# Attention scores in column tiles of 32 keys, with later queries only, in a recurrent-attention and MoE kernel

## The chip, the cores and the metric

One core of a Trainium2 chip runs the whole program. The metric is device time in microseconds (us) of that core; the kernel before took 594.9 us (median of 3 runs, 594.86 to 596.61). TensorE (PE in the profile) multiplies matrices into PSUM, VectorE (DVE), ScalarE (ACT) and GpSimd (POOL) work on tiles, and the sync engine (SP) issues the DMA transfers.

## The reference

Stage one is a linear recurrence with a complex decay, for 4 batches, 8 heads, 768 steps and 48 dimensions; stage two is a feed-forward layer over all 3072 tokens.

```
for t in range(S):
    new_re = ar * S_re - ai * S_im          # ar, ai: normalised decay of step t
    new_im = ar * S_im + ai * S_re
    S_re, S_im = new_re + outer(k[t], v[t]), new_im
    y[t] = q[t] @ S_re
x = y, heads side by side                   # [3072, 384]
h = x @ w_in                                # [3072, 2048]
g = maximum(h, 0) + log1p(exp(-abs(h)))
out = g @ w_out                             # [3072, 384]
```

The kernel computes stage one in 24 chunks of 128 steps (6 groups of steps times 4 batches). Within a chunk, query t sees key s only where s <= t, so the matrix of scores is triangular; what lies before the chunk comes in through a state.

## The kernel before

**Per chunk and in order.** `pre` turns the decays into logarithms and angles (ACT and DVE), sums them along the steps (matmuls L508 for the first group, scans L491 later), and multiplies q and k with the resulting powers; DMAs L603 and L607 copy q and k into the tile qk, with the 96 real and imaginary parts of a head on the partitions. `chunk` then does, for each of the 24 chunks:

- transposes of k (PE L622), evacuated by ACT (L629, L631);
- scores (PE L647): for each of 8 heads one f32 matmul of 128 keys by 128 queries, four heads into one PSUM bank, so two halves of four matmuls;
- the mask (DVE L650): each half times a 128x128 triangle of ones, into the tile a;
- the output y (PE L678 from the state, L681 from a and v): 16 matmuls each, of 32 columns of weights, four of them side by side in the array's four column tiles;
- the new state (PE L703, in three column tiles, and DVE L712).

**The feed-forward layer.** `moe` runs per group of 512 tokens: for each of 16 slices f of d_ff, nine matmuls of 512 columns into h (L738), then Abs, Exp, Ln on ACT (L743 to L745), three DVE operations (L746, L748, L750; the second also on ACT, L749), and nine matmuls into three accumulators o (L762). A tile is split into a rounded part and a rest (gh and gl, xh and xl), hence nine instead of three. There are 96 groups of nine of each kind. From here on a group means nine such matmuls.

**A check.** `inspect` loads both weights once more in 32 pieces (seen), takes their absolute value (ACT L393) and sums up a bound (ACT L394); `judge` then weighs all the bounds (DVE L863 to L867), adds them up with a 1x1 matmul pn (PE L871) and so decides whether a slower general path is needed. It isn't here.

**What sets the order.** Nothing is ordered by the program text: every operation is a task with a cost, dependencies and a key from the table `K`, and `Planner.order` plays the engines through and writes out one order per engine, which the engines follow strictly. Where PE has nothing ready before the first group of L762, the planner writes a filler, a matmul of the identity (L798), so that PE's clock stays up. The number of fillers is thus fixed when the program is built.

Of the kernel before, what the change touches and what calls it, by code (L numbers as in the profile page):

```python
# [11 lines left out]
F32 = mybir.dt.float32  # L12
# [4 lines left out]
ALU = mybir.AluOpType  # L17
# [4 lines left out]
P = 128  # L22
B, H, S, D = 4, 8, 768, 48
# [5 lines left out]
CH = 128  # L29
# [14 lines left out]
KVT = 32  # L44

# [18 lines left out]
class Buf:  # L64
    def __init__(self, pool, tag, shape, dtype, name, bufs=1):
# [5 lines left out]
    def __call__(self):  # L71
        if self.obj is None:
            self.obj = self.pool.tile(self.shape, self.dtype, tag=f"{self.tag}_{self.slot}", name=self.name, bufs=1)
        return self.obj


class Task:
    __slots__ = ("eng", "dur", "fn", "key", "idx", "deps", "outs", "bufs", "tab", "nbytes", "left", "ready", "end", "alt")

    def __init__(self, eng, dur, fn, key, idx, tab, nbytes):  # L80
        self.eng, self.dur, self.fn, self.key, self.idx, self.tab, self.nbytes = eng, dur, fn, key, idx, tab, nbytes
        self.deps, self.outs, self.bufs, self.end = set(), [], [], 0.0
        self.alt = {}


class Planner:
    WIN = 3.4133
    FREE = 0.2
    LAT = {"ACT": {"ACT": 0.14, "DVE": 0.14, "PE": 0.15, "POOL": 0.1, "SP": 0.1},
# [45 lines left out]
    def order(self, filler, until, gate):  # L135
# [36 lines left out]
        table = "log"  # L172
        out = []
# [3 lines left out]
        while done < n:  # L177
# [20 lines left out]
            for e in engines:  # L198
# [4 lines left out]
                for t in pend[e] + (alts[e] if e in alts else []):  # L203
                    if t.ready > now:
                        nxt = t.ready if nxt is None else min(nxt, t.ready)
                        continue
                    if not room(t):
                        continue
                    if e == "SP" and dma_free > now + K["backlog"]:
                        nxt = dma_free - K["backlog"] if nxt is None else min(nxt, dma_free - K["backlog"])  # L210
                        continue
                    if t.eng != e:
                        work = max(0.0, free[t.eng] - now) + sum(
                            u.dur for u in pend[t.eng] if u.ready <= now and (u.key, u.idx) < (t.key, t.idx))
                        if work + t.dur < t.alt[e][0] + K["altpen"]:
                            continue
                    k = t.key + (K["tpen"] if t.tab and t.tab != table else 0.0)
                    if best is None or (k, t.idx) < best[0]:
                        best = ((k, t.idx), t)
                if best is None and e == "PE" and ends and gate.end and not until.end:  # L220
                    t = Task("PE", 0.214, filler, 0, -1, None, 0)
                    free[e] = now + self.array(now, t.dur)
# [22 lines left out]
                if e == "PE":  # L245
                    dur = self.array(now, dur)
# [31 lines left out]
class Prog:  # L278
# [15 lines left out]
    def consts(self):  # L294
# [4 lines left out]
        self.mask = c.tile([P, P], F32, tag="mask", name="mask")  # L299
        nc.gpsimd.memset(self.mask, 1.0)  # L300
        nc.gpsimd.affine_select(
            out=self.mask, in_=self.mask, pattern=[[1, P]], base=0,
            channel_multiplier=-1, compare_op=ALU.is_ge, fill=0.0,
        )
# [93 lines left out]
    def pre(self, si):  # L398
# [176 lines left out]
    def chunk(self, si, c):  # L575
# [13 lines left out]
        vt = self.vt[gc]  # L589
# [47 lines left out]
        am = []  # L637
        for j in range(2):
# [29 lines left out]
        def ymm():  # L668
            yy, q, v = y(), qk(), vt()
# [14 lines left out]
        add("PE", 1.19 if first else 2.38, ymm, at(), r=[qk, vt] + am + ([] if first else [sp]), w=[y])  # L684
# [9 lines left out]
        if not last:  # L694
# [11 lines left out]
            add("PE", 0.95, kvmm, at("state"), r=[kt, vt], w=[kv])  # L706
# [93 lines left out]
    def fast(self):  # L800
        with ExitStack() as ctx:
# [3 lines left out]
            self.x, self.vt = {}, {}  # L805
# [151 lines left out]
    def tokens(self):  # L957
# [78 lines left out]
    "judge": 3656.994,  # L1036
    "head": [
        2361.764, 90.426, 186.918, 828.6, -1179.026, 1665.811, 853.645, 122.5, 210.292, 299.959,
        2514.528, 765.795, 773.157, 1145.396,
    ],  # L1040
    "turn": [
        -1513.703, 2539.75, 283.981, -99.814, 144.317, 2815.741, 2230.689, 133.705, 205.779, 204.008,
        499.374, 774.09, 741.541, 373.819,
    ],
    "tail": [
        -5848.997, 383.858, -1999.396, -642.154, -5.741, 2629.094, 285.386, 132.423, 999.968, 189.692,
        228.801, 4092.001, 4909.0, 4392.766,
    ],
    "chunk": [
        -918.284, -524.779, 2957.251, 1802.451, 205.193, 104.187, 2951.945, 1167.349, 960.729, 1177.829,  # L1050
        4197.869, 270.781, 852.91, 259.323, 2229.167, 587.025, 439.879, 286.542, 2159.076, 855.741,
        1181.943, 2905.977, 1810.108, 1955.233,
    ],
    "state": [
        -3231.394, -1499.995, -99.254, -124.602, 43.116, 43.124, 88.757, 55.237, 128.405, 128.491,
        135.783, 136.063, 199.792, 140.866, 242.533, 203.435, 281.062, 250.568, 287.24, 301.809,
        -219.968, 2830.189, 43.882, -576.403,
    ],
    "wgt": [
        -470.753, -1307.379, 346.43, -3791.449, -3420.177, -1988.745, 2456.441, 389.871, 1190.129,  # L1060
        117.907, 129.074, 312.459, 123.09, 417.712, 146.793, 741.91,
    ],
    "moe": [
        31.451, 83.853, 132.162, 198.126, 302.101, 1104.311, 4399.954,
    ],
    "step": [
        4.077, 3.163, 2.754, 6.265, 4.251, 185.005, 1662.331,
    ],
    "seen": 116.978,
    "seenstep": 583.073,  # L1070
    "rlead": 357.33,
    "xlead": -5880.358,
    "vlead": -78.682,
    "plead": -5.114,
    "backlog": 1.983,
    "altpen": -0.151,
    "tpen": 10.226,
# [19 lines left out]
def _layout(q, k, v, a_re, a_im, moe_w_in, moe_w_out):  # L1097
# [23 lines left out]
    vpad = np.ascontiguousarray(vp.reshape(B, NGRP, CH, VW).transpose(2, 1, 0, 3).reshape(CH, NCHUNK, VW))  # L1121
# [20 lines left out]
```

## Time and profile before

| | |
|---|---|
| median of 3 runs | 594.9 us |
| profiled execution | 595.1 us |
| its span | 593.3 us |
| PE busy | 573.6 us, 97% of the span |
| weight loads (PEld) busy | 477.9 us, 81% |
| DVE busy | 438.2 us, 74% |
| ACT busy | 439.4 us, 74% |
| HBM read, written | 50.33 MB, 5.51 MB |

The span runs from the first to the last instruction of the program; 1.8 us of the profiled execution's time lie around it. A matmul's busy time in the profile overlaps with the next one's, so what a matmul costs PE is read from start to start. An f32 matmul leaves two records in the trace, an fp32r one (L738, L762) one.

### The profile page before, as it was taken

The page shows a single profiled execution, that of the slowest core. Times are in us where ns is not written, and L with a number is a line of the kernel's source. Part 1 is how long each engine was busy: PE and PEld are TensorE (multiplying, and loading weights), DVE is VectorE, ACT ScalarE, POOL GpSimd, SP SyncE. Part 2 cuts the span into 40 slices and gives each one's busy share as a digit, 9 for nine tenths or more (in the row PEclk, how much of TensorE's full clock was granted, in tenths as well). Part 3 has the DMA queues.
Part 4 walks back from the last instruction along what each step waited for, and adds up shares of the span by engine and source line. Part 5 has one row for each costly group of instructions (what it writes and reads, how often), then busy time and mean ns, then how long its engine had stood idle before and what let it go on. Part 6 is the DMA issues. An engine that isn't in the chain of part 4 may idle for free.

```text
span 593.3 us, 12166 instructions
## 1 busy us (share of the span) xinstructions
PE 573.6 (97%) x4984; PEld 477.9 (81%) x4984; DVE 438.2 (74%) x676; ACT 439.4 (74%) x770; POOL 1.8 (0%) x16
## 2 busy tenths in 40 slices
PE   1999999999999999999999999999999999999995
PEld 1999988887887888788888888888888877788884
DVE  6998998978997999886967978877735335443432
ACT  7987688658989597858859668699549899365452
POOL 1000000000000000000000000000000000000000
PEclk9999999999999999999999999999999999999999
DMA  8899743424002527244431434510329973010001
GB/s 325 345 299 297 304 123 124 112 75 155 1 0 68 163 74 225 69 128 156 124 123 29 111 124 108 176 43 27 81 60 301 296 223 110 2 53 1 0 1 57
DMA packets 42237, 75.55 MB, mean 127 GB/s; under 512 B 3520, under 2 KB 26560, under 8 KB 42176
## 3 DMA queue, kind: packets, MB, share of 16 engines
q1 hardware_dynamic: 42176, 74.73, 40.7%
q8 instruction: 40, 0.66, 0.5%
q14 instruction: 21, 0.17, 0.1%
HBM read 50.33 MB, written 5.51 MB: 94 GB/s over the span
## 4 chain that ended last, share of the span: by engine, by line
PE 74%; DVE 11%; ACT 9%; DMA 3%; issue 1%; SPq 1%; DVEq 0%; ACTq 0%
PE h L738 27%; PE o L762 26%; PE o L798 6%; PE sc L647 5%; PE y L681 2%; PE kv L703 2%; PE y L678 2%; PE tr L622 2%; DVE lt L746 2%; PE sum L508 1%; DVE gl L750 1%; DMA seen<-w_out_dram 1%; DVE a L650 1%; DVE x L531 1%; ACT L850 1%
## 5 line engine op out<-in xcount | busy, mean ns | idle before, releaser
L738 PE MATMUL h<-xt,wi 128*128 128x512 f32 x864 | 218.8, 399 | 0.8 <-DVE lt L746 0.7
L762 PE MATMUL o<-gh,wo 128*128 128x512 f32 x576 | 198.0, 400 | 0.0
L738 PEld LDWEIGHTS h<-xt,wi 128*128 128x128 f32 x864 | 159.7, 188 | 38.1 <-DVE lt L746 1.9
L746 DVE SCALAR_TENSOR_TENSOR lt<-h,lt 128x512 f32<-128x512 f32 x96 | 66.1, 689 | 99.3 <-ACT lt L745 99.1
L762 PEld LDWEIGHTS o<-gh,wo 128*128 128x128 f32 x576 | 108.4, 188 | 25.7 <-issue 1.2
L743 ACT ACTIVATE lt<-h 128x512 f32<-128x512 f32 x96 | 56.7, 592 | 81.9 <-PE h L738 81.4
L762 PE MATMUL o<-gl,wo 128*128 128x512 f32 x288 | 113.8, 395 | 0.1
L745 ACT ACTIVATE lt<-lt,one 128x512 f32<-128x512 f32 x96 | 69.5, 724 | 2.2
L750 DVE TENSOR_TENSOR gl<-lt,gh 128x512 fp32r<-128x512 f32 x96 | 66.2, 689 | 2.2 <-ACT gh L749 0.6
L762 PEld LDWEIGHTS o<-gl,wo 128*128 128x128 f32 x288 | 54.3, 188 | 12.1 <-DVE gl L750 0.6
L744 ACT ACTIVATE lt<-lt 128x512 f32<-128x512 f32 x96 | 60.6, 631 | 2.0
L647 PE MATMUL sc<-qk 96*128 96x128 f32 x384 | 48.4, 278 | 0.3 <-DVE a L650 0.3
L647 PEld LDWEIGHTS sc<-qk 96*128 96x128 f32 x384 | 46.2, 191 | 3.0 <-DVE a L650 0.7
L798 PE MATMUL o<-ident 128*128 128x128 f32 x334 | 40.3, 278 | 0.0
L798 PEld LDWEIGHTS o<-ident 128*128 128x128 f32 x334 | 39.1, 194 | 0.2 <-issue 0.2
L650 DVE TENSOR_TENSOR a<-sc,mask 128x512 f32<-128x512 f32 x48 | 32.2, 684 | 9.4 <-PE sc L647 9.2
L491 DVE TENSOR_TENSOR_SCAN t<-hold,t 128x384 f32<-128x384 bf16 x40 | 36.1, 945 | 1.1 <-DMA out_dram<-o 0.4
L850 ACT ACT_TABLE_LOAD x28 | 35.9, 1283 | 0.4
L749 ACT ACTIVATE gh<-lt 128x512 fp32r<-128x512 f32 x40 | 25.2, 630 | 11.3 <-DVE lt L746 7.1
L748 DVE TENSOR_SCALAR gh<-lt 128x512 fp32r<-128x512 f32 x56 | 23.9, 426 | 3.9
L681 PE MATMUL y<-a,v 128*32 128x128 f32 x768 | 25.9, 273 | 0.0
L564 DVE TENSOR_TENSOR x<-x,t 128x768 f32<-128x768 f32 x24 | 22.3, 952 | 4.3 <-ACT t L538 4.2
(88 smaller groups left out, 607.4 us busy)
## 6 DMA issues: line engine op xcount, KB each, us to landing
x<-dense_dram SPq DMA_DIRECT2D x20, 768.0 KB, 5.8
qk<-x SPq DMA_DIRECT2D x48, 288.0 KB, 4.2
raw_wo<-w_out_dram SPq DMA_DIRECT2D x8, 768.0 KB, 10.0
raw_wi<-w_in_dram SPq DMA_DIRECT2D x8, 768.0 KB, 7.8
seen<-w_in_dram SPq DMA_DIRECT2D x16, 384.0 KB, 4.3
seen<-w_out_dram SPq DMA_DIRECT2D x16, 384.0 KB, 3.8
v<-vpad_dram SPq DMA_DIRECT2D x24, 224.0 KB, 2.6
qk<-x SPq DMA_DIRECT2D x48, 96.0 KB, 3.9
```

Source lines behind the costliest of these rows:

```text
L647: PE.matmul(psc()[:, hh * P : (hh + 1) * P], q[:, h, CH:], q[:, h, :CH], start=True, stop=True)
L650: V.tensor_tensor(a(), psc().rearrange("p (h t) -> p h t", h=4), self.mask[:, None, :].to_broadcast([P, 4, P]), ALU.mult)
L681: PE.matmul(o(G), v[:, w : w + 32], am[h // 4]()[:, h % 4, :], start=first and prim and G < 4, stop=not prim)
L738: PE.matmul(h()[:, :n], w()[:, q, i, fs], x()[:, i, :n], start=k == 0, stop=k == 3 * NI - 1)
L743: add("ACT", a1(n) - 0.04, lambda: A.activation(tv(), h(), AF.Abs), k, r=[h], w=[t])
L744: add("ACT", a1(n), lambda: A.activation(tv(), tv(), AF.Exp, scale=-1.0), k, w=[t], tab="log")
L745: add("ACT", a1(n, 1), lambda: A.activation(tv(), tv(), AF.Ln, bias=self.one), k, w=[t], tab="log")
L746: add("DVE", d1(n), lambda: V.scalar_tensor_tensor(tv(), h(), 0.0, tv(), ALU.max, ALU.add), k, r=[h], w=[t])
L750: add("DVE", d1(n), lambda: V.tensor_tensor(gl(), tv(), gh().bitcast(F32), ALU.subtract), k, r=[t, gh], w=[gl])
L762: PE.matmul(acc[m]()[:, :n], w()[:, wq, f % 2, ms], x(), start=f == f0 and q == 0, stop=f == f1 - 1 and q == 2)
L798: self.nc.tensor.matmul(self.acc0[0]()[:, :P], self.ident, x, start=True, stop=True)
L850: nc.scalar.preload_act_table_set(TABLES[table])
```

## The change

A half of the scores (four heads) becomes 16 matmuls instead of four. The 128 keys are cut into quarters of 32, and each quarter goes to one column tile of the array, which writes 32 partitions of PSUM. For a quarter that begins at key lo, only the queries from lo on are computed: 128, 96, 64 or 32 columns. So that each column tile gets one matmul of each length, the quarters are turned by one place per head: column tile t of head r holds the quarter (t + r) mod 4. The matmuls of a half are issued in the order in which they would start if each tile ran its own ones back to back.

The rows of a are then turned per head. The mask becomes four triangles (`tri`, 128 x 4 x 128), one for each turn, and y needs v with its rows turned in the same way: the host adds such a copy to vpad, and it is loaded as a tile vr of its own, for all 24 chunks; the plain v is loaded for the 20 chunks that update the state. Columns that no score matmul writes keep what the bank held, which the mask multiplies by zero; the three banks are cleared once at the start. y's matmuls read vr; the state's matmuls are as before.

The planner now knows PE operations in column tiles (`cols`): entering them costs 0.19 us in its plan, and it has other costs for scores, y and the state. All keys in `K` are new.

```diff
+KR = 32
+NROT = P // KR
...
+        self.tri = c.tile([P, NROT, P], F32, tag="tri", name="tri")
+        for r in range(NROT):
+            t = self.tri[:, r]
...
+            sel(out=t, in_=t, pattern=[[0, P]], base=KR * r - P, channel_multiplier=1, compare_op=ALU.is_ge, fill=0.0)
+            sel(out=t, in_=t, pattern=[[1, P]], base=P - KR * r, channel_multiplier=-1, compare_op=ALU.is_ge, fill=0.0)
+            sel(out=t, in_=t, pattern=[[-1, P]], base=KR * r - 1, channel_multiplier=1, compare_op=ALU.is_ge, fill=1.0)
...
-            add("SP", 0.45, lambda vt=vt, gc=gc: nc.sync.dma_start(vt(), self.vpad[:, gc, :]),
-                K["chunk"][gc] - K["vlead"], w=[vt], nbytes=4 * VW * P)
+            vr = self.vr[gc] = Buf(p, "vr", [P, VW], F32, f"vr{gc}", 2)
+            if not last:
+                add("SP", 0.45, lambda vt=vt, gc=gc: nc.sync.dma_start(vt(), self.vpad[:, gc, :VW]),
+                    K["state"][gc] - K["vlead"], w=[vt], nbytes=4 * VW * P)
+            add("SP", 0.45, lambda vr=vr, gc=gc: nc.sync.dma_start(vr(), self.vpad[:, gc, VW:]),
+                K["chunk"][gc] - K["vlead"], w=[vr], nbytes=4 * VW * P)
...
+        order = sorted((sum(CH - KR * ((t + x) % NROT) for x in range(r)), t, r)
+                       for t in range(NROT) for r in range(NROT))
...
-                for hh in range(4):
-                    h = 4 * j + hh
-                    PE.matmul(psc()[:, hh * P : (hh + 1) * P], q[:, h, CH:], q[:, h, :CH], start=True, stop=True)
+                for _, t, r in order:
+                    lo = KR * ((t + r) % NROT)
+                    PE.matmul(psc()[KR * t : KR * t + KR, r * P + lo : (r + 1) * P],
+                              q[:, NROT * j + r, CH + lo : CH + lo + KR], q[:, NROT * j + r, lo:CH],
+                              start=True, stop=True)
...
-                V.tensor_tensor(a(), psc().rearrange("p (h t) -> p h t", h=4),
-                                self.mask[:, None, :].to_broadcast([P, 4, P]), ALU.mult)
+                V.tensor_tensor(a(), psc().rearrange("p (h t) -> p h t", h=NROT), self.tri, ALU.mult)
...
-            add("PE", 0.9, score, at(), r=[qk], w=[psc])
+            add("PE", 0.54, score, at(), r=[qk], w=[psc]).cols = True
...
-            yy, q, v = y(), qk(), vt()
+            yy, q, v = y(), qk(), vr()
...
+            for j in range(NATT):
+                t = Buf.fixed["att", j] = self.ps.tile([P, 512], F32, tag=f"att_{j}", name=f"att{j}")
+                self.nc.vector.memset(t, 0.0)
...
-    "judge": 3656.994,
+    "judge": 10301.974,
```

In numbers the order changes as follows. PE has 768 score matmuls instead of 192, and 185 fillers instead of 167. PE goes from another kind of work into column tiles 56 times instead of 42, and between f32 matmuls of the whole array and groups of 512 columns 41 times instead of 79. ACT rounds gh 61 times instead of 40, DVE 35 times instead of 56. SP has 20 loads of v more.

The first place is PE at the second chunk, before: its scores (sc), the fillers (o from ident), and y from a and v.

```order
L647 MATMUL sc_0_494<-qk_357 128x128 x4
L647 MATMUL sc_1_502<-qk_357 128x128 x4
L798 MATMUL o_158<-ident 128x128 x19
L681 MATMUL y_547<-a_0_521,v_189 32x128 x6
L681 MATMUL y_547<-a_1_539,v_189 32x128 x6
```

The same place now: the end of the second half of the scores (att is the bank that holds them), the fillers, and the beginning of y.

```order
L675 MATMUL att_118<-qk_372 32x128
L675 MATMUL att_118<-qk_372 32x64
L675 MATMUL att_118<-qk_372 32x96
L675 MATMUL att_118<-qk_372 32x64
L675 MATMUL att_118<-qk_372 32x32
L827 MATMUL o_182<-ident 128x128 x8
L710 MATMUL att_116<-a_0_552,vr_221 32x128 x6
L710 MATMUL att_116<-a_1_561,vr_221 32x128 x6
```

Sixteen rows of four lengths stand for each half, and between scores and y there are 8 fillers instead of 19.

The second place is ACT at the end of the check, before: the last pieces of seen and the Abs, Exp and Ln of one slice f (lt).

```order
L393 ACTIVATE seen_5226<-seen_5226 128x384
L745 ACTIVATE lt<-lt,one 128x512
L394 ACTIVATE seen_5226,chk<-seen_5226,wlim 128x384
L393 ACTIVATE seen_5245<-seen_5245 128x384
L393 ACTIVATE seen_5265<-seen_5265 128x384
L394 ACTIVATE seen_5245,chk<-seen_5245,wlim 128x384
L394 ACTIVATE seen_5265,chk<-seen_5265,wlim 128x384
L393 ACTIVATE seen_5304<-seen_5304 128x384
L394 ACTIVATE seen_5304,chk<-seen_5304,wlim 128x384
L743 ACTIVATE lt<-h 128x512
```

And the same place now.

```order
L772 ACTIVATE lt<-h 128x512
L416 ACTIVATE seen_5831,chk<-seen_5831,wlim 128x384
L773 ACTIVATE lt<-lt 128x512
L415 ACTIVATE seen_5852<-seen_5852 128x384
L774 ACTIVATE lt<-lt,one 128x512
L416 ACTIVATE seen_5852,chk<-seen_5852,wlim 128x384
L415 ACTIVATE seen_5856<-seen_5856 128x384
L415 ACTIVATE seen_5873<-seen_5873 128x384
L416 ACTIVATE seen_5856,chk<-seen_5856,wlim 128x384
L416 ACTIVATE seen_5873,chk<-seen_5873,wlim 128x384
L772 ACTIVATE lt<-h 128x512
```

The pieces of seen stand closer together now. From the tenth Abs before the last row above to the last L416, ACT's order has 10 triples Abs, Exp, Ln, 26 of L415 and 27 of L416. That tenth Abs belongs to the slice that PE computes just before the last chunk's y; from there to the 1x1 matmul of the check (L903) PE's order has that y and 21 groups.

The third place is SP before the third and fourth chunk's q and k, before the change.

```order
L341 DMA raw_wi_437<-w_in_dram 128x1536
L458 DMA x_455<-dense_dram 128x2x768 x2
L341 DMA raw_wi_508<-w_in_dram 128x1536
L464 DMA v_529<-vpad_dram 128x448
L603 DMA qk_536<-x_101 96x1x768 x2
L607 DMA qk_536<-x_101 96x1x256 x2
L464 DMA v_584<-vpad_dram 128x448
L603 DMA qk_588<-x_101 96x1x768 x2
```

And now.

```order
L363 DMA raw_wo_441<-w_out_dram 128x1536
L480 DMA x_488<-dense_dram 128x2x768 x2
L490 DMA vr_583<-vpad_dram 128x448
L490 DMA vr_589<-vpad_dram 128x448
L363 DMA raw_wo_598<-w_out_dram 128x1536
L629 DMA qk_619<-x_125 96x1x768 x2
L633 DMA qk_619<-x_125 96x1x256 x2
L629 DMA qk_647<-x_125 96x1x768 x2
```

Up to the fourth chunk's q and k the order had 11 loads of weights and 4 of v; now it has 9 of weights and 8 of v (four plain, four turned).

## Rows read from the trace of the kernel before

**Rows 1.** The page: span, and busy time, share and instructions of PE.

```profile
span 593.3 us, 12166 instructions
PE 573.6 (97%) x4984; PEld 477.9 (81%) x4984; DVE 438.2 (74%) x676; ACT 439.4 (74%) x770; POOL 1.8 (0%) x16
```

**Rows 2.** Waits of PE: line waited for, us in total, times, longest us.

```profile
PE sum L508 <- DVE t L482: 11.9, 1, 11.9
PE h L738 <- DVE lt L746: 0.7, 2, 0.5
```

**Rows 3.** Two stretches: busy us of PE, PEld, DVE, ACT, POOL; clock; DMA share; GB/s.

```profile
12.00:85.00 73.00, 73.00 (x874) 69.52 (x877) 69.94 (x110) 59.86 (x108) 0.00 (x0) 1.00 0.83 288
440.00:500.00 60.00, 59.53 (x500) 48.46 (x489) 26.42 (x48) 54.72 (x131) 0.00 (x0) 1.00 0.81 245
```

**Rows 4.** PE in order of time, 192.7 to 210: start us, us, line, tiles, xcount.

```profile
192.68 2.36 PE L738 MATMUL h<-xt,wi 128*128 128x512 f32 x9
194.88 1.95 PE L647 MATMUL sc<-qk 96*128 96x128 f32 x16
196.59 2.34 PE L738 MATMUL h<-xt,wi 128*128 128x512 f32 x9
198.86 1.08 PE L678 MATMUL y<-qk,s 96*32 96x128 f32 x32
199.75 1.06 PE L681 MATMUL y<-a,v 128*32 128x128 f32 x32
200.63 0.96 PE L703 MATMUL kv<-v,kt 128*32 128x64 f32 x48
201.53 0.51 PE L762 MATMUL o<-gh,wo 128*128 128x512 f32 x1
...
208.60 1.06 PE L681 MATMUL y<-a,v 128*32 128x128 f32 x32
209.59 0.73 PE L738 MATMUL h<-xt,wi 128*128 128x512 f32 x2
```

**Rows 5.** The chain that ended last, in order of time: start us, us, what.

```profile
18.45 8.04 PE o L798 x72
...
85.23 2.29 PE o L762 x9
...
150.29 2.09 PE h L738 x9
```

**Rows 6.** DMA issues of v: xcount, KB each, median us to landing.

```profile
v<-vpad_dram SPq DMA_DIRECT2D x24, 224.0 KB, 2.6
```

**Rows 7.** POOL and ACT in order of time, near the start.

```profile
1.43 0.29 POOL L301 TENSOR_SCALAR_AFFINE_SELECT mask<-mask 128x128 f32<-128x128 f32 x1
...
8.09 0.60 ACT L476 ACTIVATE x<-x,one 128x384 f32<-128x384 f32 x1
```

**Rows 8.** ACT in order of time, within the check.

```profile
486.50 0.60 ACT L743 ACTIVATE lt<-h 128x512 f32<-128x512 f32 x1
486.97 0.67 ACT L394 ACTIVATE seen<-seen,wlim 128x384 f32<-128x384 f32 x1
...
487.59 0.66 ACT L744 ACTIVATE lt<-lt 128x512 f32<-128x512 f32 x1
488.12 0.58 ACT L393 ACTIVATE seen<-seen 128x384 f32<-128x384 f32 x1
488.55 0.76 ACT L745 ACTIVATE lt<-lt,one 128x512 f32<-128x512 f32 x1
489.16 0.67 ACT L394 ACTIVATE seen<-seen,wlim 128x384 f32<-128x384 f32 x1
```

**Rows 9.** ACT's group L393 by line: xcount, busy us, mean ns, idle us before.

```profile
L393 ACT ACTIVATE seen<-seen 128x384 f32<-128x384 f32 x32 | 17.0, 556 | 2.1 <-DMA seen<-w_in_dram 1.2 <-DMA seen<-w_out_dram 0.9
```

**Rows 10.** DVE and PE in order of time, at the check's end.

```profile
499.93 0.23 DVE L867 TENSOR_REDUCE sum<-chk 128x1 f32<-128x72 f32 x1
...
506.88 0.19 PE L871 MATMUL pn<-one,sum 128*1 128x1 f32 x2
```

More of the change, by code (lines that the diff above doesn't have):

```diff
@@ L71, in __call__ @@
     def __call__(self):
+        if self.obj is None and (self.tag, self.slot) in self.fixed:
+            self.obj = self.fixed[self.tag, self.slot]
         if self.obj is None:
@@ L77 @@
 class Task:
-    __slots__ = ("eng", "dur", "fn", "key", "idx", "deps", "outs", "bufs", "tab", "nbytes", "left", "ready", "end", "alt")
+    __slots__ = ("eng", "dur", "fn", "key", "idx", "deps", "outs", "bufs", "tab", "nbytes", "left", "ready", "end", "alt",
+                 "cols")
     def __init__(self, eng, dur, fn, key, idx, tab, nbytes):
@@ L217, in order @@
                     k = t.key + (K["tpen"] if t.tab and t.tab != table else 0.0)
+                    if e == "PE" and t.cols != cols:
+                        k += K["cpen"]
                     if best is None or (k, t.idx) < best[0]:
@@ L245, in order @@
                 if e == "PE":
+                    if t.cols and not cols:
+                        dur += self.TURN
+                    cols = t.cols
                     dur = self.array(now, dur)
@@ L298, in consts @@
         make_identity(nc, self.ident)
[L299 to L304, printed above, removed]
+        self.tri = c.tile([P, NROT, P], F32, tag="tri", name="tri")
+        for r in range(NROT):
+            t = self.tri[:, r]
+            sel = nc.gpsimd.affine_select
+            nc.gpsimd.memset(t, 1.0)
+            if not r:
+                sel(out=t, in_=t, pattern=[[1, P]], base=0, channel_multiplier=-1, compare_op=ALU.is_ge, fill=0.0)
+                continue
+            sel(out=t, in_=t, pattern=[[0, P]], base=KR * r - P, channel_multiplier=1, compare_op=ALU.is_ge, fill=0.0)
+            sel(out=t, in_=t, pattern=[[1, P]], base=P - KR * r, channel_multiplier=-1, compare_op=ALU.is_ge, fill=0.0)
+            sel(out=t, in_=t, pattern=[[-1, P]], base=KR * r - 1, channel_multiplier=1, compare_op=ALU.is_ge, fill=1.0)
+        self.mask = self.tri[:, 0]
         self.one = self.const("one", 1.0)
@@ L704, in kvmm @@
                                   start=h == 0, stop=h == H - 1)
-            add("PE", 0.95, kvmm, at("state"), r=[kt, vt], w=[kv])
+            add("PE", 0.74, kvmm, at("state"), r=[kt, vt], w=[kv]).cols = True
             kvv = lambda: kv()[: 2 * D, :VW]
@@ L1062 @@
+        1894.062, 222.242, 77.362, 100.293, 4952.173, 467.811, 120.991,
     ],
     "moe": [
[L1064 removed]
+        21.432, 70.631, 122.941, 201.699, 303.615, 3786.706, 6068.826,
     ],
     "step": [
[L1067 removed]
+        5.81, 4.051, 9.176, 8.13, 89.212, 587.044, 4838.315,
     ],
[L1069 to L1077, printed above, removed]
+    "seen": 539.849,
+    "seenstep": 5661.898,
+    "rlead": 5.448,
+    "xlead": -15783.598,
+    "vlead": -3544.785,
+    "plead": -672.2,
+    "backlog": 1.627,
+    "altpen": -6.424,
+    "tpen": 18.921,
+    "cpen": 0.0,
     "table": 1.3,
@@ L1120, in _layout @@
     vp[:, :, VP - D :] = vt[:, 1::2]
-    vpad = np.ascontiguousarray(vp.reshape(B, NGRP, CH, VW).transpose(2, 1, 0, 3).reshape(CH, NCHUNK, VW))
+    vp = vp.reshape(B, NGRP, CH, H // 2, VP).transpose(2, 1, 0, 3, 4).reshape(CH, NCHUNK, H // 2, VP)
+    vr = np.zeros_like(vp)
+    for h in range(H):
+        c = slice(0, VP - D) if h % 2 == 0 else slice(VP - D, VP)
+        vr[:, :, h // 2, c] = np.roll(vp[:, :, h // 2, c], -KR * (h % NROT), axis=0)
+    vpad = np.ascontiguousarray(np.concatenate([x.reshape(CH, NCHUNK, VW) for x in (vp, vr)], 2))
     wi = np.ascontiguousarray(moe_w_in.reshape(NI, P, NWP, WCOL).transpose(1, 2, 0, 3))
```

40 lines of the change are left out of this document (22 added, 18 removed).

## The prediction

> **What bounds the kernel now.** I read the page's first part, then who makes PE wait, then stretches, then single starts. PE is busy for 97% of the span [rows 1]. It waits once before its first matmul, 11.9 us for DVE, and then hardly ever: the longest other line is 0.7 us [rows 2]. Between 12 and 85 us PE shows 73.00 of 73.00 us busy, but part of that is fillers, 72 records in one piece of the chain [rows 3, 5]; DVE is busy for 69.94 of the same 73 us, so there DVE and the work that feeds it set the pace and the fillers stand in PE's gaps [rows 3]. From the first L762 at 85.23 us [rows 5] to the end there are no fillers, and PE's own work is the bound. So the time is the first wait, plus the sum of what PE's order holds, fillers included, plus the last stores; the change acts through that sum, and a new wait of PE is added in full.
>
> **Scores.** Before, the 16 records of a chunk (both halves) begin at 194.88 and the next group at 196.59: 1.71 us a chunk, 0.855 a half [rows 4], and 24 x 1.71 = 41.0 us for all chunks. The trace has no score matmul in column tiles, but y and the state run there. In y 32 records of 128 columns take 0.89 us (198.86 to 199.75), eight on each of the four tiles, so 8a + 1024b = 0.89, with a for a record and b for a column. In the state 48 records, 16 on each of three tiles, take 0.90 us (200.63 to 201.53), of which 0.10 is the way out of the column tiles (below): 16a + 896b = 0.80. Together b = 0.85 ns and a = 2.5 ns or so. A new half has eight records and 2 x 320 columns on each tile: 0.57 us. The spread from the two rows is small: y's rate per column alone gives 0.556, the state's rate per record (0.80 / 48 x 32) 0.533, the same with the 0.10 left in 0.60. But in both rows the matmuls side by side are equally long, and the new ones are not; if tiles had to wait for each other, a half takes 0.945 us (the rival below). I take 0.57, as each f32 matmul leaves two records on its tile, 0.11 us each, and yet 32 records need only 27.8 ns each: a tile's second record does not hold up the other tiles' first. So 48 x (0.855 - 0.57) = 13.7 us less.
>
> A rule of the Trainium skill speaks against the short ones: TensorEngine Tiling, section Instruction Overhead, says that a matmul of one column takes as long as one of about 60. By it the 32-column matmuls would count 60, a tile 2 x 348 columns, a half 0.605 us at 0.87 ns, and the forecast would be 1.9 us higher. The rows differ from it, as far as they go: with the state's 48-column records counted as 60, its stretch would take 0.86 us at y's rate, and took 0.80 [rows 4]. No run before has 32 columns.
>
> **Ways in and out.** A group takes 2.09 us [rows 5]. Ahead of scores it takes 2.20 (192.68 to 194.88), ahead of y 2.27 (196.59 to 198.86); y ahead of a group takes 0.99 (208.60 to 209.59) instead of 0.89 [rows 4]. So going into column tiles from a group costs 0.18, out of them 0.10, and between f32 in the whole array and a group 0.10. PE goes in 14 times more and out 14 times more, +3.9 us, and 38 times less between the other two, -3.8. Net 0, within 1 us.
>
> **Fillers.** 72 records take 8.04 us [rows 5], a filler 0.223. 18 more: +4.0 us. This is what the plan gives back of the four chunks before the first L762, where PE isn't the bound.
>
> **Mask, v, constants.** The mask multiplies 512 elements by 512 as before; its price is taken as unchanged. The rounding of gh moves 21 operations from DVE to ACT, neither of which PE waits for after 85 us; it matters in the next paragraph only. The 20 more loads of v have 224 KB each [rows 6], 4.5 MB. Where DMA is tight, in the first 85 us at 0.83 of its time and 288 GB/s [rows 3], the order up to the fourth chunk's q and k has four loads of v more, 0.9 MB, and two of weights less (768 KB each, 1.5 MB), so 0.6 MB less. Taken at 0; if that cover fails, 0.9 MB at 288 GB/s are 3 us. POOL's nine more selects at 0.29 us and three shorter memsets, some 3 us, stand ahead of the constants, which ACT first reads at 8.09 us [rows 7]: the old mask is done by 1.72 us, the new ones by about 5, so 0. The clearing of three banks stands ahead of DVE's first operation, while the first loads fly: 0.
>
> **The wait that comes.** With PE faster, the check's end comes closer to PE. Before, DVE's last step of it starts at 499.93 and pn runs at 506.88 [rows 10]: over 6 us to spare. Now ACT has, over the stretch described with the order, 10 triples and 26 and 27 halves of seen. From start to start an Abs takes 0.47 us, an Exp 0.53, a Ln 0.61, L393 0.43, L394 0.62 [rows 8]: 16.1 + 11.2 + 16.7 = 44.0 us, plus about 0.9 for DVE's steps and the hand-overs (an estimate from L867's 0.23 and its few small neighbours): 44.9. PE's 21 groups and the y take 21 x 2.09 + 1.78 + 0.28 = 46.0. So 1 us is left if ACT never waits, and ACT did wait 2.1 us for pieces of seen [rows 9]; ACT ran at 54.72 of 60 us there [rows 3]. I take 1 us of waiting at the 1x1 matmul, with 0 and 4 as ends.
>
> **Sum**, against the profiled execution's 595.1 us: 595.1 - 13.7 + 4.0 + 0 + 1.0 = 586.4 us. The median of the runs is 594.9, so this is about -1.4%. Its own range: the half between 0.533 and 0.60 gives -1.8 to +1.4, the ways in and out 1 either way, the wait -1 to +3, loads up to +3: 583 to 591.
>
> **Rivals.**
>
> *The tiles wait for each other (slower).* If matmuls start and end in their order of issue, the mixed lengths lose: following the issue order, each of four rounds lasts as long as its 128-column member, and a 32-column one is left over, 544 columns instead of 320. A half takes 2 x 544 x 0.87 ns = 0.945 us, 0.09 more than before: +4.3 + 4.0 = 603.4 us, and the wait at the check vanishes, since PE comes later. It decides from 0.77 us a half on, where 48 x (0.855 - 0.77) no more pays for the fillers. For it: no row shows unequal lengths side by side. Against it: the two records of one matmul do not hold up the others, as said. The Trainium skill has a rule of this kind: TensorE: Matmul & The Clock Gate, Part 3, says under what overlaps that matmuls are in program order in start and end. By that rule this rival is the forecast; no run here shows it for unequal lengths.
>
> *Early waits take it back.* Up to the first L762 the order asks DVE for the second chunk's mask sooner (8 fillers instead of 19 between scores and y, 2.5 us), and DVE has 3 us of slack in 73 [rows 3]. If DVE, ACT or the loads come later than planned, PE idles, behind it all that follows. Against it: in the kernel before the same planner's order left PE no wait after the first [rows 2]. Price: 3 us of slack, 3 us of loads: 592.4.
>
> *The check holds PE longer.* If seen's pieces come late as well as ACT, the 1x1 matmul waits 4 us and more instead of 1, and with it the group behind it on PE: 590 to 593.
>
> *More is saved.* Half scores at 0.533, no wait: 595.1 - 15.5 + 4.0 = 583.6, or some less with cheaper ways in.
>
> **Numbers.** Forecast 0.64, the early waits 0.10, the check 0.08, more saved 0.06, tiles that wait 0.12. What a measurement can tell from no change is 0.3%, 1.8 us, so faster means under 593.1: the forecast, more saved, and most of the two waits, 0.83. Within 0.3%: 0.05. Slower: the tiles that wait and a worse sum of waits, 0.12. Between 582.5 and 595 lie the forecast, the waits and most of the rest: a little over 0.8.
>
> **What would show it.** In the profile after: the 64 score records of a chunk in 1.1 to 1.2 us from start to start (0.57 a half; 0.95 would be the first rival); 370 records of fillers; the first group of L762's line near 85 us as before; among PE's waits a line for the 1x1 matmul on DVE of 0 to 4 us, and no line over 2 us other than it and the first; DVE's mask at its old duration. The forecast is wrong if PE's idle time after 12 us comes to more than 5 us, or if the stretch of a half is over 0.65 us.

## The result and the profile after

The changed kernel took 587.31 us (median of 4 runs, 586.28 to 587.64) against 594.88 us before: ratio 0.9863, 95% interval [0.9841, 0.9884]. Forecast were 586.4 us. Run a second time at the end of the study it took 587.84 us (5 runs), ratio 0.9867 [0.9844, 0.9891].

The page's first part, which answers to [rows 1]: PE is busy for 8.6 us less in a span 7.5 us shorter; the 1188 records more are the short score matmuls and 36 records of fillers (18 fillers, two records each).

```profile
span 585.8 us, 14565 instructions
PE 565.0 (96%) x6172; PEld 465.2 (79%) x6172; DVE 430.2 (73%) x659; ACT 447.6 (76%) x790; POOL 4.4 (1%) x28
```

PE's waits after, as in [rows 2]: line waited for, us in total, times, longest us. The first is the old one. New are two pauses with no releaser ("issue"), 1.0 us in the scores (L675) and 0.8 in y (L710). The 0.8 for lt are one wait of a group of h for DVE, from 463.3 us on; [rows 2] has 0.7 for lt, in two waits. There is no line for the check's 1x1 matmul.

```profile
PE sum L534 <- DVE t L508: 11.9, 1, 11.9
PE att L675 <- issue: 1.0, 1, 1.0
PE att L710 <- issue: 0.8, 1, 0.8
PE h L767 <- DVE lt L775: 0.8, 1, 0.8
PE sum L534 <- ACT t L559: 0.5, 1, 0.5
```

Beside the lines of [rows 2] the kernel before had one more wait, for a mask:

```profile
PE sc L647 <- DVE a L650: 0.3, 1, 0.3
```

The two stretches of [rows 3] after, columns as there. DVE is still busy for nearly all of the first; PE is no longer at 100% in it, by the two pauses and the 0.5. In the second ACT has 55.98 of 60 us.

```profile
12.00:87.00 75.00, 72.71 (x1054) 68.79 (x1055) 69.16 (x109) 56.48 (x103) 0.00 (x0) 1.00 0.88 294
440.00:500.00 60.00, 59.22 (x538) 47.83 (x538) 26.81 (x49) 55.98 (x134) 0.00 (x0) 1.00 0.75 227
```

PE in order of time (start us, us, line, tiles, xcount, idle before), which answers to [rows 4, 5]. The 64 records of a chunk's scores go from 195.69 to 196.95, 1.26 us instead of 1.71, and that holds the 0.10 us that the prediction found for the way out of the column tiles. The group ahead takes 2.29 (193.40 to 195.69) instead of 2.20. The first L791, the line that was L762, comes at 87.16 instead of 85.23. The rows at 39.39 and 60.49 show the pauses, each in the middle of an uninterrupted run of column-tile matmuls.

```profile
38.18 0.42 PE L710 MATMUL att<-a,vr 128*32 128x128 f32 x6
39.39 0.93 PE L710 MATMUL att<-a,vr 128*32 128x128 f32 x25 [0.79 <-issue]
...
58.76 0.75 PE L675 MATMUL att<-qk 96*32 96x128 f32 x28
60.49 0.64 PE L675 MATMUL att<-qk 96*32 96x128 f32 x23 [0.97 <-issue]
...
87.16 0.39 PE L791 MATMUL o<-gh,wo 128*128 128x512 f32 x1
...
193.40 2.36 PE L767 MATMUL h<-xt,wi 128*128 128x512 f32 x9
195.69 1.32 PE L675 MATMUL att<-qk 96*32 96x128 f32 x64
196.95 2.36 PE L767 MATMUL h<-xt,wi 128*128 128x512 f32 x9
...
499.98 0.19 PE L903 MATMUL att<-one,sum 128*1 128x1 f32 x2
```

The check's end, which answers to [rows 10]: DVE's last step starts at 498.76 and takes 0.23, and PE runs the 1x1 matmul at 499.98 (above) without waiting; of the 7 us between them 1.2 are left.

```profile
498.76 0.23 DVE L899 TENSOR_REDUCE sum<-chk 128x1 f32<-128x72 f32 x1
```

By line after: the mask at 684 ns, as before; ACT's Abs of seen with 4.3 us idle ahead of it where [rows 9] had 2.1.

```profile
L680 DVE TENSOR_TENSOR a<-att,tri 128x512 f32<-128x512 f32 x48 | 31.4, 684 | 3.2 <-PE att L675 3.1
L415 ACT ACTIVATE seen<-seen 128x384 f32<-128x384 f32 x32 | 16.4, 547 | 4.3 <-DMA seen<-w_in_dram 3.7 <-DMA seen<-w_out_dram 0.6
```

Adding up, for every PE record, the time from its start to the next one's start gives where the 7.5 us are (us, from the two traces; the last matmul and the check's are in the sums alone):

```
                          before    after   difference
up to the first matmul     11.95    11.87     -0.1
to the first group of o    73.22    75.29     +2.1
  fillers and sums         46.44    50.37     +3.9  (0.5 of wait in it)
  scores, 8 halves          7.55     6.39     -1.2  (0.97 of pause in it)
  the rest                 19.23    18.53     -0.7  (0.79 of pause in it)
to the last matmul's end  501.57   492.78     -8.8
  scores, 40 halves        34.56    25.71     -8.9
  groups of h              199.67   200.77    +1.1  (waits: 0.7 before, 0.8 after)
  groups of o              206.37   206.36      0   (waits: 0.3 before, none after)
  y, state, transposes      60.46    59.42    -1.0
after it                    6.56     5.82     -0.7
```

### The profile page after: what moved, and what is told of

Same layout as the page of the kernel before. It is cut to its first block, busy times and chain, and to the rows that moved or that the text cites. A ratio compares the mean times of both kernels' runs of the same rounds, so it can differ in the third digit from the quotient of the medians.

```text
span 585.8 us, 14565 instructions
## 1 busy us (share of the span) xinstructions
PE 565.0 (96%) x6172; PEld 465.2 (79%) x6172; DVE 430.2 (73%) x659; ACT 447.6 (76%) x790; POOL 4.4 (1%) x28
## 4 chain that ended last, share of the span: by engine, by line
PE 91%; ACT 5%; DMA 1%; issue 1%; DVE 0%; SPq 0%; ACTq 0%
PE h L767 34%; PE o L791 34%; PE o L827 6%; PE att L675 5%; PE att L710 3%; PE att L707 3%; PE att L732 3%; PE att L648 2%; DMA seen<-w_out_dram 1%; ACT seen L416 1%; ACT L882 1%; ACT seen L415 1%; DMA x<-dense_dram 1%; PE sum L534 1%; ACT x L500 0%
## 5 line engine op out<-in xcount | busy, mean ns | idle before, releaser
L791 PE MATMUL o<-gh,wo 128*128 128x512 f32 x576 | 197.2, 400 | 0.0
L767 PEld LDWEIGHTS h<-xt,wi 128*128 128x128 f32 x864 | 159.8, 188 | 38.6 <-DVE lt L775 1.4
L791 PEld LDWEIGHTS o<-gh,wo 128*128 128x128 f32 x576 | 108.3, 188 | 26.6 <-issue 1.4
L791 PE MATMUL o<-gl,wo 128*128 128x512 f32 x288 | 113.6, 394 | 0.0
L791 PEld LDWEIGHTS o<-gl,wo 128*128 128x128 f32 x288 | 54.3, 188 | 11.7 <-DVE gl L779 0.2
L778 ACT ACTIVATE gh<-lt 128x512 fp32r<-128x512 f32 x61 | 38.3, 629 | 26.3 <-DVE lt L775 18.0
L827 PE MATMUL o<-ident 128*128 128x128 f32 x370 | 45.2, 279 | 0.0
L827 PEld LDWEIGHTS o<-ident 128*128 128x128 f32 x370 | 43.2, 194 | 0.7 <-issue 0.4
L675 PEld LDWEIGHTS att<-qk 96*32 96x32 f32 x1536 | 29.7, 110 | 6.2 <-issue 5.2
L675 PE MATMUL att<-qk 96*32 96x96 f32 (+3 forms) x1536 | 33.3, 235 | 1.0 <-issue 1.0
L680 DVE TENSOR_TENSOR a<-att,tri 128x512 f32<-128x512 f32 x48 | 31.4, 684 | 3.2 <-PE att L675 3.1
L590 DVE TENSOR_TENSOR x<-x,t 128x768 f32<-128x768 f32 x24 | 22.1, 953 | 13.7 <-ACT t L564 13.7
L710 PE MATMUL att<-a,vr 128*32 128x128 f32 x768 | 25.9, 273 | 0.8 <-issue 0.8
L710 PEld LDWEIGHTS att<-a,vr 128*32 128x32 f32 x768 | 21.3, 110 | 1.5 <-issue 1.1
```

The source lines that it names most:

```text
L675: PE.matmul(psc()[KR * t : KR * t + KR, r * P + lo : (r + 1) * P], q[:, NROT * j + r, CH + lo : CH + lo + KR], q[:, NROT * j + r, lo:CH], ...
L710: PE.matmul(o(G), v[:, w : w + 32], am[h // 4]()[:, h % 4, :], start=first and prim and G < 4, stop=not prim)
L767: PE.matmul(h()[:, :n], w()[:, q, i, fs], x()[:, i, :n], start=k == 0, stop=k == 3 * NI - 1)
L778: x.alt["ACT"] = (a1(n), lambda: A.activation(gh(), tv(), AF.Copy))
L791: PE.matmul(acc[m]()[:, :n], w()[:, wq, f % 2, ms], x(), start=f == f0 and q == 0, stop=f == f1 - 1 and q == 2)
L827: self.nc.tensor.matmul(self.acc0[0]()[:, :P], self.ident, x, start=True, stop=True)
```

## The experiments

Theory: PE's own sum decides, a half costs 0.57 us because the column tiles run unequal matmuls side by side, and the new order gives some of it back in fillers. Main rival: the tiles wait for each other. In the cuts of code below, "..." stands for lines or parts of lines left out. The times of before shown beside the runs lay between 595.1 and 595.7 us.

**The short stream.** Every quarter meets all 128 queries; nothing else changes.

```diff
-                    PE.matmul(psc()[KR * t : KR * t + KR, r * P + lo : (r + 1) * P],
-                              q[:, NROT * j + r, CH + lo : CH + lo + KR], q[:, NROT * j + r, lo:CH],
+                    PE.matmul(psc()[KR * t : KR * t + KR, r * P : (r + 1) * P],
+                              q[:, NROT * j + r, CH + lo : CH + lo + KR], q[:, NROT * j + r, :CH],
```

> The changed kernel's order and column tiles, but every quarter of the keys meets all 128 queries. If the gain comes from the shorter streams (each column tile runs its own matmuls back to back): a half of the scores 0.89 us instead of 0.57, like y, 48 x 0.32 = +15.4 us, 601 to 603 us, slower than the kernel before. If the gain comes from the new order, or from working side by side in four tiles whatever the length: no change, 586 to 589 us.

602.78 us (599.79 to 603.44), ratio 1.0101 [1.0057, 1.0144]: slower than before. A chunk's scores there (PE in order of time):

```profile
200.29 1.98 PE L675 MATMUL att<-qk 96*32 96x128 f32 x64
202.20 2.36 PE L767 MATMUL h<-xt,wi 128*128 128x512 f32 x9
```

1.91 us, 0.905 a half without the way out. So 1024 columns a tile (both records of a matmul counted) instead of 640 cost 0.327 us a half more, 0.852 ns a column, y's rate, and 0.03 us a half is left over for the rest. All of the gain of a half is in the columns that are left out; column tiles alone lose (0.905 against 0.853 before).

**One part without the other.** First the new order and the new loads with the old scores:

```diff
-                for _, t, r in order:
-                    lo = KR * ((t + r) % NROT)
-                    PE.matmul(psc()[KR * t : KR * t + KR, r * P + lo : (r + 1) * P], ...
+                for hh in range(4):
+                    h = 4 * j + hh
+                    PE.matmul(psc()[:, hh * P : (hh + 1) * P], q[:, h, CH:], q[:, h, :CH], start=True, stop=True)
...
```

> The changed kernel's order on every engine and its loads, but the scores are four matmuls of 128 x 128 a half again (with the one triangle as mask, and v not turned in the second copy). Scores theory: 48 x (0.855 - 0.57) = +13.7, fewer ways into and out of the column tiles about cancel against the change between f32 and groups, so 599 to 601 us, more than the kernel before. Order theory (the new plan, not the scores, made the time): under 591 us.

596.08 us (10 runs), ratio 1.0016 [1.0000, 1.0032]: 8.8 above the changed kernel, less than expected. Start to start its scores take 42.97 us on PE against 32.10 (1.0 of it a pause), 10.9 more and not 13.7, since the 32.10 hold ways out of the column tiles too. Groups of o are 1.5 us shorter, groups of h 1.1 (no wait for lt), y 0.5 (no pause). The order and the loads alone gain nothing.

Then the new scores in the old order (the planner's costs and its table K as before), 167 fillers, v and turned v in one load:

```diff
-            vt = self.vt[gc] = Buf(p, "vt", [P, VW], F32, f"v{gc}", 2)
-            vr = self.vr[gc] = Buf(p, "vr", [P, VW], F32, f"vr{gc}", 2)
...
+            vt = self.vt[gc] = self.vr[gc] = Buf(p, "vt", [P, 2 * VW], F32, f"v{gc}", 2)
+            add("SP", 0.45, lambda vt=vt, gc=gc: nc.sync.dma_start(vt(), self.vpad[:, gc, :]), ...
...
 K = {   # the table of the kernel before
```

> The kernel before, in its own order on every engine and with its own 167 fillers, but with the new scores; one load brings v and turned v together (448 KB instead of 224). If PE's sum is all there is: -13.7, +0.8 for 17 more ways in and out and 40 fewer changes between f32 and groups: 582 us, 5 us below the changed kernel, and the new order costs rather than helps. Rival: the old plan counted 0.9 us a half, so other engines can't follow, PE waits at the masks and at lt, and 586 to 592 us come out, with new lines among PE's waits that sum up to the difference.

595.45 us (10 runs), ratio 0.9997 [0.9977, 1.0017]: nothing gained, 13 us above the 582 of PE's sum. PE's waits there, beside its first (columns as above):

```profile
PE att L728 <- DMA v<-vpad_dram: 2.2, 1, 2.2
PE h L763 <- DVE lt L771: 2.1, 2, 1.7
PE o L787 <- DVE gl L775: 1.2, 2, 0.6
PE att L706 <- DVE a L676: 0.8, 1, 0.8
PE att L671 <- DVE a L676: 0.6, 1, 0.6
```

The scores have shrunk by 10.7 us there too (42.11 to 31.37). Start to start, groups of o have grown by 5.2, fillers and sums by 3.3, groups of h by 1.3: PE arrives earlier, and what it needs has not been moved up.

The same with v loaded as before:

```diff
-            ... Buf(p, "vt", [P, 2 * VW], F32, f"v{gc}", 2)
-            ... nc.sync.dma_start(vt(), self.vpad[:, gc, :])
+            ... Buf(p, "vt", [P, VW], F32, f"v{gc}", 2)
+            ... nc.sync.dma_start(vt(), self.vpad[:, gc, :VW])
...
-            yy, q, v = y(), qk(), vr()[:, VW:]
+            yy, q, v = y(), qk(), vr()
```

> The new scores in the old order, as in the run before, but with v loaded as before (one load of 224 KB a chunk, y reads v unturned, which is left out of the work). If that run's shortfall against 582 us (PE's sum without 18 fillers) came from its double loads of v, PE's wait of 2.2 us for v and what follows it go: 590 to 593 us. Rival: PE, now ahead, waits for DVE's and ACT's steps in an order that was planned for the longer scores: waits of the same size at other places, 594 to 595.5 us. The plain sum of PE's work says 582.

592.91 us (10 runs), ratio 0.9961 [0.9938, 0.9983]. Each beside its own times of before, this is some 2 us better, the part of my double loads; 11 us above PE's sum remain, and groups of o are still 5.0 us longer than before. The wait for v is still there (1.3 us), and DVE's a, lt and gl hold PE for 4.7 us in all. Neither part alone reaches the 7.6 us.

**The order in which a half's matmuls are issued.** The changed kernel sorts the 16 matmuls of a half by the columns already given to their tile. Here they go tile by tile, four in a row on one:

```diff
-        order = sorted((sum(CH - KR * ((t + x) % NROT) for x in range(r)), t, r)
-                       for t in range(NROT) for r in range(NROT))
+        order = [(0, t, r) for t in range(NROT) for r in range(NROT)]
```

> The changed kernel with the 16 score matmuls of a half issued tile by tile (four in a row on one tile) instead of interleaved; same matmuls, same columns on each tile, 0.557 us. If every tile took its own work from far ahead, nothing changes: 587.3 us, half 0.57. If PE starts matmuls in the order of issue and a tile that is busy holds up those behind it, a tile starts only when the last matmul of the one before it has started: a half takes the 128, 96, 64 and 32 columns less the last of each tile, between 1.3 and 1.8 us, and the time is 587.3 + 48 x (0.75 to 1.2) = 623 to 645 us.

623.84 us (623.02 to 624.95), ratio 1.048 [1.0449, 1.0511]. PE in order of time:

```profile
206.72 2.90 PE L674 MATMUL att<-qk 96*32 96x128 f32 x64
209.55 2.36 PE L766 MATMUL h<-xt,wi 128*128 128x512 f32 x9
```

2.83 us a chunk, 1.365 a half on average, within what waiting in the order of issue was expected to cost. The starts of the single records say how far PE runs ahead. A tile has eight records in a half. In the first half the fifth of the first tile starts at 207.128 us and the next tile's first at 207.133; the same pair comes at 207.435 and 207.441, at 207.637 and 207.643, and, from the last tile to the second half, at 207.948 and 207.954. So a tile holds its running record and three more, that is one whole matmul behind the running one, and the next one for that tile holds up all that were issued after it.

The expectation below reads 1.365 us as 1600 columns, the time of a half by itself; that this fits is luck. The second half starts 1.23 us after the first, before the first one ends, so that by this rule the two take 1280 and 1600 columns, 2.46 us; the first record of each tile takes some 0.03 us beyond its columns (0.133 instead of 0.110 for 128), 0.2 us for the eight; with the way out that makes 2.8. The rule was then tried on another order, in rounds of four tiles:

```diff
+        order = [(0, t, r) for r in range(NROT) for t in range(NROT)]
```

> The changed kernel with the 16 score matmuls of a half issued in rounds (one on each of the four tiles, then the next four) instead of by the columns already issued to a tile; same matmuls. The run tile by tile took 1.365 us a half. That is 1600 columns at 0.853 ns, which comes out if PE hands matmuls out in the order of issue, and a tile takes one in while another runs on it; with none taken in ahead it would be 2048 columns, 1.75 us, and with free tiles 640, 0.55 us. For the rounds the same three ways give 352 x 2 columns (0.60 us a half; +0.055 x 48 = 590 us), 448 x 2 (0.765; 597 us) and 320 x 2 (0.57; 587.3 us).

588.62 us (588.05 to 590.1), ratio 0.9894 [0.9877, 0.9912]. The time lies between two of the three cases; the duration is plainer:

```profile
194.78 1.40 PE L674 MATMUL att<-qk 96*32 96x128 f32 x64
196.11 2.36 PE L766 MATMUL h<-xt,wi 128*128 128x512 f32 x9
```

1.33 us, 0.07 more than the 1.25 of the changed kernel. For two halves back to back, one matmul taken in ahead gives 64 columns more than free tiles (0.05 us), none taken in 320 more (0.27 us). One ahead fits both runs; the sorted order comes to 640 columns a half whether a tile takes in one matmul or all of them, so it pays nothing.

**The loads of turned v.** First without the 20 early ones:

```diff
-            add("SP", 0.45, lambda vr=vr, gc=gc: nc.sync.dma_start(vr(), self.vpad[:, gc, VW:]),
+            add("SP", 0.45, lambda vr=vr, gc=gc: last and nc.sync.dma_start(vr(), self.vpad[:, gc, VW:]),
-            yy, q, v = y(), qk(), vr()
+            yy, q, v = y(), qk(), (vr if last else vt)()
```

> The changed kernel without its 20 loads of turned v (224 KB each, 4.5 MB): y of the first 20 chunks reads v unturned, the last four keep theirs; the order of the rest stays. The prediction priced the loads at 0: 587.3 us within 0.5. Rival, loads up to 3 us as their upper end said: 584 to 586 us, with fewer waits before 87 us.

624.6 us (623.59 to 625.57), ratio 1.0481 [1.045, 1.0511]: 37 us slower with less to load, which neither theory had. The edit had a second effect. y now reads the plain v, whose two buffers stay taken until y, and the next load of v waits for them at the head of SP's queue. SP in order of time, the changed kernel first, then this run, the same three places of the queue (v, two loads of weights, the inputs x):

```profile
55.18 0.34 SPq L488 DMA_DIRECT2D v<-vpad_dram  x1
56.24 0.81 SPq L363 DMA_DIRECT2D raw_wi<-w_in_dram  x2
61.51 0.38 SPq L480 DMA_DIRECT2D x<-dense_dram  x1
```

```profile
73.05 0.35 SPq L488 DMA_DIRECT2D v<-vpad_dram  x1
73.50 1.85 SPq L363 DMA_DIRECT2D raw_wi<-w_in_dram  x2
75.52 0.38 SPq L480 DMA_DIRECT2D x<-dense_dram  x1
```

The y before it on PE ran at 71.91 for 1.08 us: v's load starts as it ends, 18 us late, and x 14 us late. DVE, which needs x, then leaves PE waiting (PE in order of time):

```profile
88.48 1.92 PE L710 MATMUL att<-a,v 128*32 128x128 f32 x30 [9.27 <-DVE a L680]
```

Part of the 37 us is PE's clock. After PE had stood still for 9.27 us, the 32 records of this y took 2.02 us (88.48 to 90.50) instead of some 0.9 [rows 4], and the granted clock of the stretch around it was 0.78, a mean over time at 2.4 and at 1.2 GHz (columns as in [rows 3]):

```profile
75.00:98.00 23.00, 13.73 (x112) 12.44 (x111) 13.27 (x18) 11.21 (x16) 0.00 (x0) 0.78 0.57 205
```

PE's waits after its first come to 31 us against 3.1 in the changed kernel; that leaves some 10 us of the spans' difference to the lower clock and smaller things, an estimate. So the run says nothing on the price of a load. Another edit keeps the two buffers of turned v, fills each once, and loads no more into them up to the last group:

```diff
+            def turned(vr=vr, gc=gc):
+                if last or vr.slot not in self.held:
+                    self.held.add(vr.slot)
+                    nc.sync.dma_start(vr(), self.vpad[:, gc, VW:])
...
+            for j in range(2):
+                Buf.fixed["vr", j] = self.p.tile([P, VW], F32, tag=f"vr_{j}", name=f"vr{j}")
...
```

> The changed kernel with the first load of turned v into each of its two buffers, and none after them up to the last four chunks: 18 loads of 224 KB fewer, y of chunks 2 to 19 reads the turned v of another chunk. Unlike the run without turned v, no buffer of the plain v is held longer. The prediction priced the loads at 0: 587.3 us within 1. Rival, their upper end of 3 us: 584 to 586 us.

587.04 us (585.65 to 589.22), ratio 0.986 [0.9837, 0.9882]: the loads cost nothing that can be measured when they have a pair of buffers of their own.

**The fillers.** Every tenth is left out:

```diff
+            count = iter(range(1, 10000))
+            filler = lambda: next(count) % 10 and self.filler(self.ident)
...
```

> The changed kernel without every tenth filler: 167 instead of 185, as many as before. The prediction charged 4.0 us for the 18 more, as part of PE's own sum. If that holds, 587.3 - 4.0 to 583.3 us and no new wait of PE. Rival: the fillers stand in gaps that DVE leaves, and PE waits there instead: 587 us, with 3 to 4 us of new waits for DVE before 87 us.

587.14 us (585.89 to 589.71), ratio 0.9865 [0.9841, 0.9889]: the rival's time. PE's waits beside the first:

```profile
PE att L710 <- DVE a L680: 1.5, 1, 1.5
PE sum L534 <- ACT t L559: 1.3, 1, 1.3
PE att L710 <- issue: 1.2, 1, 1.2
PE att L675 <- issue: 1.1, 1, 1.1
...
PE att L732 <- ACT kt L655: 0.5, 1, 0.5
```

Waits for DVE and ACT in the early stretch rise from 0.5 to 3.3 us; the first group of o comes at 85.84 instead of 87.16, and later waits (a pause of 1.2 us in a y at 276 us, 0.6 us for qk at 369) take that back. So of the 4.0 us some 2.8 are room that DVE and ACT need; a shorter list of fillers alone does not win it.

**The two pauses.** In the trace a 16 KB packet of a queue of the kind "instruction" starts at 37.2 and at 57.9 us and takes 0.98 and 1.12; PE goes on some 1.2 to 1.5 us after it ends. That queue has 40 such packets in the kernel before and 49 in the changed one, one for some 250 records of PE and PEld in both, which points to PE's own code. Two runs make the stream of instructions thinner near there. Four fillers as one matmul of 512 columns:

```diff
+        for _ in range(n // 4):
+            self.nc.tensor.matmul(acc.rearrange("p (a b) -> p a b", a=4), self.ident,
+                                  self.ident[:, None, :].to_broadcast([P, 4, P]), start=True, stop=True)
+        for _ in range(n % 4):
+            self.nc.tensor.matmul(acc[:, :P], self.ident, self.ident, start=True, stop=True)
...
```

> The changed kernel, but of each run of fillers every four are one matmul of 512 columns, so as long, with a quarter of the instructions. For the two pauses of PE of 1 us without a waited-for engine, at 38 and 59 us. If they are PE's code not being there in time (a 16 KB load of instructions lands about 1.2 us before PE goes on in both): less code to load in that stretch, one or both pauses go or shrink, 585 to 586.5 us. If they belong to the column tiles or the scores themselves: both stay, 587 us.

586.93 us (584.97 to 587.86), ratio 0.9846 [0.9806, 0.9886]: both pauses gone, but waits of 1.8 us for the DMA of qk at 367 us and 0.5 for lt stand in their place, and the time is that of the changed kernel.

```profile
PE att L675 <- DMA qk<-x: 1.8, 1, 1.8
PE h L767 <- DVE lt L775: 0.5, 1, 0.5
```

And the first four chunks with whole-array scores:

```diff
+                if first:
+                    for r in range(NROT):
+                        PE.matmul(psc()[:, r * P : (r + 1) * P], q[:, NROT * j + r, CH:], q[:, NROT * j + r, :CH],
+                                  start=True, stop=True)
+                    return
...
```

> The changed kernel, with the scores of the first four chunks again as 128x128 matmuls in the whole array (and their v not turned): 8 halves at 0.855 instead of 0.57 us, +2.3 us, and 192 records of scores fewer before 90 us. If the two pauses of PE at 38.6 and 59.5 us (2.0 us together, beside packets of PE's instructions) come from the denser stream of small instructions there, both go and the time is 587.3 + 2.3 - 2.0 = 587.6 us. Rival: the pauses come from something else in the order and stay: 589.6 us.

590.42 us (589.41 to 591.15), ratio 0.9917 [0.9888, 0.9945], nearest to the rival's 589.6: the two early pauses are gone, but one of 0.7 us stands in a y at 241 us and 0.7 us of waiting for qk at 370. The third run was the changed kernel itself:

> The changed kernel once more, unaltered. If its two pauses of PE (0.8 and 1.0 us, nothing waited for, each behind a packet of instructions) belong to places of the program, its profile shows them again near 39 and 60 us and the time is 587.3 us. If they depend on what else the DMA engines carry at that moment, they show at other places or not at all, and the time differs by less than 2 us.

587.84 us. PE's waits beside the first:

```profile
PE att L710 <- issue: 1.8, 1, 1.8
PE att L675 <- DMA qk<-x: 1.0, 1, 1.0
PE h L767 <- DVE lt L775: 0.6, 2, 0.4
```

One pause of 1.8 us at 43.7 instead of two at 38.6 and 59.5: they are no fixed places of the program. The traces of all runs have eleven pauses of 0.3 us and more without a releaser. All stood in column-tile code (scores or y), and the kernel before and the run with the old scores showed none. Each of the eleven ended 1.25 to 1.62 us after such a 16 KB packet had landed; but an execution has 40 to 49 such packets, and all but none to two of them passed without a pause. So late code is the likely cause, argued from this timing and not shown: no run changed the loading of the code alone.

## Why the prediction held, step by step

The mechanism, the sign and the size were right: 587.3 against 586.4, with 0.9 between them. That they came so close is in part luck, since smaller terms missed in both directions. By its terms, against the profiled execution:

- **Scores, -13.7.** A half takes 0.577 us ((1.254 - 0.10) / 2) instead of 0.853: 48 x 0.276 = 13.2. Sizing it from y and the state in [rows 4] was right: 0.85 ns a column holds for the short ones too. (The sign of 1.1 to 1.2 us a chunk came out as 1.25, because it left out the way out.)
- **Ways in and out, 0.** It came to +1.0, the end of the stated "within 1 us". The scores' rows gained 2.2 us of ways out (13.2 less 10.0 net, less the 1.0 of pause); y, state and transposes lost 0.7, 1.2 and 0.6; groups of h and o gained 1.0 and 0.3, once the waits are taken out of both traces.
- **Fillers, +4.0.** Fillers and sums grew by 3.9. But they are no price of 18 matmuls as such: without 18 the time stays. The early stretch is long because of DVE and ACT, as [rows 3] said, and the term was right only because the order had put the fillers where those need time. (The first group of o came at 87.16 us and not "near 85 us as before": that sign forgot the term.)
- **Loads, mask, constants, 0.** Right, the loads by a run of their own.
- **The wait at the check, +1.0.** There was none. DVE's last step started 1.2 us ahead of PE instead of just too late, although ACT waited 4.3 us for seen. No other wait took its place: the 0.8 for lt stand against 0.7 for lt and 0.3 for a mask before, so these waits fell by 0.2 (the 0.5 for ACT is in the fillers' row). What made up for the term in the sum is the 1.0 of the ways in and out, by luck.
- **Not foreseen.** The pauses, +1.8, and a shorter end: 0.7 us less after the last matmul, which the new order has with the old scores too (5.9 us there). The first matmul came 0.1 us sooner.

Together -13.2 + 1.0 + 3.9 - 0.2 + 1.8 - 0.7 - 0.1 = -7.5, as in the spans. The upper end of the stated range, 591, is less than the parts named for it add up to (594.8).

The rivals: the tiles that wait for each other were priced at 0.945 us a half, which would need matmuls to end in the order of issue. They are handed to the tiles in that order, as the run tile by tile shows, but with the lengths sorted that costs nothing, and a short one need not end after a long one issued before it. The Trainium skill, TensorE: Matmul & The Clock Gate, Part 3, has matmuls in program order in start and in end. The traces agree with neither for unequal lengths side by side: tile by tile the fifth matmul issued starts at 207.133 us and the fourth, which waits on its own tile, at 207.239, and a half at 0.577 us rules out an end in order; the measurement decides.

Against a price for short matmuls: on one tile the next record starts 0.028 to 0.032 us after one of 32 columns, and the 384 columns that the first run adds cost 0.852 ns each. By the floor of about 60 columns that the Trainium skill has (TensorEngine Tiling, Instruction Overhead) the step would be 0.051 us and the half, as the prediction worked out, 0.605; neither agrees.

The early waits that were to take the gain back came as 0.5 us. Where the order stayed old, waits of 6.9 us came, over the whole span.

## What to carry to other kernels

Matmuls of unequal length in column tiles run side by side if they are issued by the columns already given to each tile; issued tile by tile the same matmuls took 2.4 times as long. A faster step in a planned order was worth little (0.2 to 2.3 us of 7.6) until the order was planned for it, and an operand that is read later needs buffers of its own, or it holds the queue that loads everything else. Fillers in a stretch that another engine paces are only in small part a reserve.

## What was not expected of the hardware

- PE hands out column-tile matmuls in the order of issue, and a tile takes in one behind the running one: in the run tile by tile the next tile starts each time 0.005 to 0.006 us after the fifth of eight records of the one before. On their tiles they then start and end out of the order of issue.
- PE can stand still for 0.3 to 1.8 us within dense column-tile code with nothing waited for, at places that differ between two executions of one kernel, each time 1.25 to 1.62 us after a 16 KB packet of the instruction queue landed. What causes it stays open.
- When such a pause went away the time did not follow: in the run with wide fillers 1.8 us of waiting for qk appeared later. A gap in PE is not worth its length when other engines are that close behind.
